# Weight splitting of four experts on two engines instead of three, and a later request for the words of the next conversion

## The chip, the core and the metric

The kernel runs on one core of a Trainium2 chip. A core has five engines that run their own instruction streams in order and wait for one another by semaphores: TensorE (PE, matmuls; PEld is its weight load), VectorE (DVE), ScalarE (ACT), GpSimd (POOL) and SyncE (SP, which here issues most of the DMAs). ACT issues some DMAs from its own stream, too. The metric is the device time of one execution in microseconds (us); the time of the kernel before is the median of three runs.

## What is computed

The reference is a chain of three blocks on 1536 tokens of 512 values, all in float32:

```
attn = softmax(scale * q k^T + bias, on global and local columns) v      # 2 x 8 heads, 768 x 64
x    = attn as (1536, 512)
e(i) = argmax(x w_gate); gate = softmax(x w_gate)[e(i)]                  # 8 experts, capacity 384
x[i] = gate * relu(x[i] w1[e(i)]) w2[e(i)]                               # 512 -> 1024 -> 512
out  = softplus(x w_in) w_out                                            # 512 -> 2048 -> 512
```

`w_in` and `w_out` arrive as 64-bit words and are turned into float32 by the kernel itself.

## The kernel before

The kernel runs three stages one after the other: attention with routing (up to about 147 us), the eight experts (147 to 358 us) and the dense layer, called m here (358 to 627 us). The order of the instructions on each engine is the order in which the Python code emits them; nothing moves them afterwards.

**Experts.** The experts run in order of their number of tokens, as use index `ui` 0 to 7, with 256, 352, 272, 240, 224, 208, 200 and 184 columns. Each has eight steps `f`. A step emits `e_stage1` (matmuls into `ps_h`, then a relu that makes the hidden tile) and then, two steps behind (`LAG = 2`), `e_stage2` (matmuls into `ps_y`). For experts 1 to 4 (`SPLIT`) every operand is held as two parts of a narrower type, a high part and a low part, and `three` (L1116 to L1118) makes three matmuls of each product. There the relu is ACT's `hs` (L1143), and DVE makes the low part of `hs` (L1144). After the last step of an expert `e_out` copies its result out: `zh` on ACT (L1174), `zl` on DVE (L1175), four each. `trans_x` transposes the next expert's tokens (`ps_xt`), with `xTs` in two parts (ACT L1110, DVE L1111).

**Splitting the weights.** Weights of experts 1 to 4 (key "s") and of the dense layer (key "m") come as 512 KB `raw` tiles, four buffers. `split` takes them in pieces of 128 x 512: the high part is a cast (`hi`, L441 or L443), the low part is `raw - hi` (L431). Four pieces make one use, which is what PE needs for two steps, a pair. In the kernel before, every fourth high part is a DVE cast (L441), the other three are ACT's (L443); every fourth low part is DVE's, the other three are POOL's. `pump` calls `split` once per step and then issues the loads of freed `raw` buffers on SP.

**Converting the words.** `conv_step` runs in every second step of the experts, in every step of the dense layer, and at heads 6 and 7 of the later attention tiles. One call stores the result of the call before the last, finishes the one before (DVE L81) and starts a new one: ACT reads the words `cr` (`csq`, L77), and DVE reads them twice (L78, L79). `cr` has three buffers. At the end of the same call `conv_load` requests the next words (L495): on ACT's queue up to the end of the experts, on SP's in the dense layer. Since the three buffers are all taken, that request goes into the buffer that the same call has just begun to read, so the engine that issues it waits for DVE's L79.

Of the kernel before, what the change touches and what calls it, by code (L numbers as in the profile page):

```python
# [72 lines left out]
def words_to_f32(nc, t, u, hi, lo, step):  # L73

    if step == 0:

        nc.scalar.activation(u, hi.bitcast(F32), AF.Abs, scale=2.0 ** -112)  # L77
        nc.vector.tensor_scalar(t, lo, 29, None, op0=ALU.logical_shift_right)  # L78
        nc.vector.scalar_tensor_tensor(t, in0=hi, scalar=-0x80000000, in1=t, op0=ALU.bitwise_and, op1=ALU.bitwise_or)  # L79
    else:  # L80
        nc.vector.scalar_tensor_tensor(t, in0=u.bitcast(I32), scalar=3, in1=t, op0=ALU.logical_shift_left, op1=ALU.bitwise_or)  # L81
# [225 lines left out]
def fast_path(ctx, tc, q, k, v, n_global, n_local, w_gate, w1, w2, cap, w_in, w_out, out, const):  # L307
    nc = tc.nc
# [113 lines left out]
    npiece, nhi = [0], [0]  # L422
    halfway = deque()

    def split(done, n):
        for _ in range(n):
            if halfway:
                raw, hi, lo, last = halfway.popleft()
                npiece[0] += 1
                eng = nc.vector if npiece[0] % 4 == 0 else nc.gpsimd  # L430
                eng.tensor_tensor(lo, raw, f32(hi), op=ALU.subtract)  # L431
                freed[0] += last
            if pending and pending[0][-1] <= done:
                raw, key, bi, k, c, _ = pending.popleft()
                if k == 0 and c.start == 0:
                    wq[key] = (wpool.tile([P, 2, NC, FQ], F32R, name="w1s", tag=f"b{bi}1", bufs=1),
                               wpool.tile([P, 2, FQ // P, DM], F32R, name="w2s", tag=f"b{bi}2", bufs=1))
                hi, lo = (wq[key][k][:, x, c, :] for x in range(2))
                nhi[0] += 1
                if nhi[0] % 4 == 0:  # L440
                    nc.vector.tensor_copy(hi, raw)  # L441
                else:
                    nc.scalar.copy(hi, raw)  # L443
                halfway.append((raw, hi, lo, c.start > 0))

    conv_done = [0]

# [5 lines left out]
    def pump(done, n, parts=1, most=NRAW):  # L453


        held[0] -= freed[0]
        freed[0] = 0
        split(done, n)
        while held[0] < most:
            if not rawq:  # L460
                if not loads_q or not ready(loads_q[0][0]):
                    return
                if loads_q[0][0][0] == "e":
                    if not parts or loads_q[0][2] > done:
                        return
                    parts -= 1
                start_load(*loads_q.popleft())
                continue
            src, key, bi, k, after = rawq.popleft()
            nb = src.shape[1]  # L470
            raw = rpool.tile([P, 1024], F32, name="raw", tag="raw", bufs=NRAW).rearrange("p (c f) -> p c f", c=nb)
            nc.sync.dma_start(raw, src)
            held[0] += 1
            for h in range(2):
                c = slice(h * nb // 2, (h + 1) * nb // 2)
                pending.append((raw[:, c, :], key, bi, k, c, after))
# [9 lines left out]
    conv_raw = deque()  # L486
# [4 lines left out]
    def conv_load():  # L491
        if conv:
            src, dst = conv.popleft()
            raw = cv.tile([P, FQ, 2], I32, name="cr", tag="cr", bufs=3)
            conv_q[0].dma_start(raw.rearrange("p n w -> p (n w)"), src)  # L495
            conv_raw.append((raw, dst))

    def conv_step(n):

        for _ in range(n):  # L500
            if conv_out:
                dst, t = conv_out.popleft()
                nc.sync.dma_start(dst, f32(t))
                conv_done[0] += 1
            if conv_now:
                dst, t, u = conv_now
                words_to_f32(nc, t, u, None, None, 1)
                conv_out.append((dst, t))
                conv_now.clear()
            if conv_raw:  # L510
                raw, dst = conv_raw.popleft()
                t = cv.tile([P, FQ], I32, name="ct", tag="cq", bufs=4)
                u = cv.tile([P, FQ], F32, name="csq", tag="cu", bufs=2)
                words_to_f32(nc, t, u, raw[:, :, 1], raw[:, :, 0], 0)
                conv_now.extend([dst, t, u])
                conv_load()


    ident = const.tile([P, P], F32, name="ident")
# [437 lines left out]
    last = len(tiles) - 1  # L957
# [13 lines left out]
    for n in range(NH + 8):  # L971
# [19 lines left out]
        if n < NH:  # L991
            if h == 1:
                load(i + 2)
            if h == (1 if i else 3):
                prep(i + 1, 0)
            if h % 2 and (i or h > 4) or i and h == 2:
                zero_fill(1)
            if h == (3 if i else 5):
                prep(i + 1, 1)
            if h == 5:  # L1000
                load_v(i + 2)
            if h == 6 and i in (2, 3, 4):
                conv_load()
            if h == 7:
                dup(i + 1)
                prev_v(i + 1)
                if i >= 5 and len(sc_q) > (i > 10):
                    scatter_x()
            if i >= 5 and h >= 6 and i < last:
                conv_step(1)  # L1010
# [174 lines left out]
    for s in range(len(steps) + LAG):  # L1185
        if s < len(steps):
            ui, f = steps[s]
            e_stage1(ui, f)
            if f in (3, 5, 6):
                trans_x(ui + 1, (3, 5, 6).index(f))  # L1190
            if f == 7 or s == 0:
                if s == 0:
                    load_order()
                load_x(ui + 1 + (f == 7))
        if s >= LAG:
            ui, f = steps[s - LAG]
            e_stage2(ui, f)
            u = part(ui, f)[0]
            if f == NFE - 1 or part(ui, f + 1)[0] != u:
                done = u  # L1200
        pump(done, 3 if s > 2 else 0, s % 2 == 0)
        if 1 <= s <= 4:
            next(routed, None)
        if s >= 6 and s % 2 == 0:
            conv_step(1)
# [78 lines left out]
    for x in range(len(plan)):  # L1284
        m_stage1(x)
        if LAG <= x < len(plan) - TAIL + LAG:
            m_stage2(x - LAG)
            if (x - LAG) % 2 == 1:
                done = plan[x - LAG][2]
        conv_step(1)  # L1290
        pump(done, 2)
        if x < NTT:
            scatter_ids(x)

        if x == 2 * NTT:
            nc.sync.dma_start(ids_row, ids_d.rearrange("(j p) o -> j (p o)", p=P))
        if x == 2 * NTT + 4:
            nc.vector.tensor_copy(ids_f, ids_row)
        if x == 2 * NTT + 5:
            ps = bank("D", "ps_ids")  # L1300
            nc.tensor.transpose(ps[:, :NTT], ids_f, ident[:NTT, :NTT])
            nc.vector.tensor_copy(ids_sb, ps[:, :NTT])
        if x == 2 * NTT + 2:
            slow = nc.values_load(slow_i[0:1, 0:1], min_val=0, max_val=1,
                                  skip_runtime_bounds_check_because="one minus a minimum of comparisons")
# [47 lines left out]
```

## Time and profile before

| | us |
|---|---|
| median of 3 runs (632.97 to 636.32) | 634.72 |
| the profiled execution | 634.79 |
| its span on the core | 633.0 |
| PE busy in the span | 606.7 |
| DVE, ACT, POOL busy | 366.9, 274.0, 171.0 |
| mean granted clock of TensorE, as a share of full speed | 0.989 |

Busy times of PE are of pipelined matmuls: a matmul of 0.27 us can start 0.11 us after the one before. A gap in PE's row is therefore a little shorter than the time that was lost. "issue" as the end of a wait means that the profile shows no other engine for it. Where rows name a line, it is that of the kernel before; from L501 on, lines of the changed kernel are up to two higher.

### The profile page before, as it was taken

The numbers are of one execution on the slowest core, as the hardware profiler recorded it, in microseconds if no ns is written. First come the engines' busy times: TensorE is split into PE (matmuls) and PEld (weight loads), VectorE is DVE, ScalarE is ACT, GpSimd is POOL, SyncE is SP. The second block draws the span as 40 slices with busy tenths as digits, with TensorE's granted clock in tenths as the row PEclk, the third lists the DMA queues.
The fourth block names the chain that finished last, engine by engine and source line by source line (L and its number), as shares of the span: only waits on it lengthen the run. The fifth ranks groups of instructions, "written<-read, shape, count | busy, mean of one in ns | idle before, by whom it ended". The sixth has DMA issues, their size and how long they took to land. (4 is left out here: it accounts for less than half of the span.)

```text
span 633.0 us, 10187 instructions
## 1 busy us (share of the span) xinstructions
PE 606.7 (96%) x3514; PEld 535.8 (85%) x3514; DVE 366.9 (58%) x1007; ACT 274.0 (43%) x600; POOL 171.0 (27%) x186
## 2 busy tenths in 40 slices
PE   6999999999999998889999999999999999999996
PEld 4899889898899997789999978888888878888874
DVE  7766888854776677733157495454577532333451
ACT  4565666743444434323253454444444433433340
POOL 4231544220755455500044241112022200100201
PEclk9999999989999999979999999999999999999998
DMA  8867778914776676779964534546422000000101
GB/s 158 225 168 215 188 213 234 316 70 134 248 229 203 213 216 191 219 262 379 376 230 133 158 71 81 134 68 80 128 66 85 2 0 1 33 34 2 50 19 70
DMA packets 92695, 93.37 MB, mean 148 GB/s; under 512 B 43314, under 2 KB 63818, under 8 KB 92634
## 3 DMA queue, kind: packets, MB, share of 16 engines
q1 hardware_dynamic: 83850, 74.53, 42.4%
q10 hardware_dynamic: 6480, 11.80, 5.5%
q0 software_dynamic: 2304, 6.30, 2.6%
q8 instruction: 30, 0.49, 0.3%
q14 instruction: 31, 0.25, 0.2%
HBM read 72.15 MB, written 20.46 MB: 146 GB/s over the span
## 5 line engine op out<-in xcount | busy, mean ns | idle before, releaser
L431 POOL TENSOR_TENSOR w1s<-raw,w1s 128x512 fp32r<-128x512 f32 x48 | 64.2, 1358 | 176.2 <-ACT w1s L443 172.0
L1228 DVE SCALAR_TENSOR_TENSOR sa<-ps_m,sa 128x512 f32<-128x512 f32 x48 | 33.1, 690 | 116.7 <-ACT sa L1227 116.7
L1225 ACT ACTIVATE sa<-ps_m 128x512 f32<-128x512 f32 x48 | 28.8, 600 | 139.8 <-PE ps_m L1118 139.8
L1116 PE MATMUL ps_m<-zh,w1s 128*128 128x512 f32 x192 | 76.1, 396 | 1.1 <-DVE sa L1228 1.1
L1117 PE MATMUL ps_m<-zl,w1s 128*128 128x512 f32 x192 | 75.7, 394 | 0.0
L1118 PE MATMUL ps_o<-w2s,g 128*128 128x512 f32 x192 | 75.7, 394 | 0.0
L1117 PE MATMUL ps_o<-w2s,g 128*128 128x512 f32 x192 | 75.5, 393 | 0.0
L1118 PE MATMUL ps_m<-zh,w1s 128*128 128x512 f32 x192 | 75.4, 392 | 0.0
L1116 PE MATMUL ps_o<-w2s,g 128*128 128x512 f32 x192 | 74.8, 389 | 0.0
L747 ACT ACTIVATE s_sb<-s_sb,negm 128x232 f32<-128x232 f32 (+1 forms) x96 | 44.0, 473 | 37.1 <-DVE negm L740 25.5
L731 PE MATMUL ps_s<-kwin,qpad 128*128 128x232 f32 (+1 forms) x192 | 55.8, 377 | 1.7 <-DVE negm L740 1.5
L1167 PE MATMUL ps_y<-h,w 128*128 128x256 f32 (+3 forms) x256 | 51.0, 343 | 0.0
L1140 PE MATMUL ps_h<-xT,w 128*128 128x256 f32 (+3 forms) x256 | 50.9, 343 | 0.0
L1140 PEld LDWEIGHTS ps_h<-xT,w 128*128 128x128 f32 x256 | 44.5, 190 | 1.9 <-ACT xT L1095 0.2
L1167 PEld LDWEIGHTS ps_y<-h,w 128*128 128x128 f32 x256 | 44.1, 190 | 1.4
L1116 PEld LDWEIGHTS ps_m<-zh,w1s 128*128 128x128 f32 x192 | 36.1, 188 | 10.7 <-DVE sa L1228 2.3
L1116 PE MATMUL ps_y<-hs,w2s 128*128 128x352 f32 (+3 forms) x128 | 39.2, 306 | 5.0 <-DVE zl L1175 5.0
L1275 POOL DMA_INDIRECT out_dram<-o,ids_sb x12 | 11.7, 973 | 117.4 <-DVE o L1270 53.3
L1117 PEld LDWEIGHTS ps_o<-w2s,g 128*128 128x128 f32 x192 | 36.0, 188 | 8.7
L1116 PE MATMUL ps_h<-xTs,w1s 128*128 128x352 f32 (+3 forms) x128 | 38.7, 302 | 4.9 <-DVE hs L1144 4.9
L1116 PEld LDWEIGHTS ps_o<-w2s,g 128*128 128x128 f32 x192 | 36.1, 188 | 8.4 <-DVE g L1235 0.3
L1118 PEld LDWEIGHTS ps_m<-zh,w1s 128*128 128x128 f32 x192 | 36.0, 188 | 8.4
(207 smaller groups left out, 1377.1 us busy)
## 6 DMA issues: line engine op xcount, KB each, us to landing
w<-in_moe_w_dram SPq DMA_DIRECT2D x16, 1024.0 KB
raw<-in_moe_w_dram SPq DMA_DIRECT2D x32, 512.0 KB
cr<-in_moe_w_in_dram ACTq DMA_DIRECT2D x24, 256.0 KB
xs_d<-early SPq DMA_DIRECT2D x22, 256.0 KB
cr<-in_moe_w_out_dram ACTq DMA_DIRECT2D x21, 256.0 KB
wi_d<-ct SPq DMA_DIRECT2D x32, 128.0 KB
wo_d<-ct SPq DMA_DIRECT2D x32, 128.0 KB
raw<-wi_d SPq DMA_DIRECT2D x8, 512.0 KB
```

Of the source, the lines that this page charges most:

```text
L431: eng.tensor_tensor(lo, raw, f32(hi), op=ALU.subtract)
L731: nc.tensor.matmul(ps[:, :w], tr[i][h % 2][:, h // 2, :], kwin[t % 2][:, h // 2, c0:], start=True, stop=True)
L747: nc.scalar.activation(pt_[n][:, :w], pt_[n][:, :w], AF.Exp, bias=negm[:, n:n + 1], scale=-1.0)
L1116: nc.tensor.matmul(ps, hi_l, hi_r, start=first, stop=False)
L1117: nc.tensor.matmul(ps, hi_l, lo_r, start=False, stop=False)
L1118: nc.tensor.matmul(ps, lo_l, hi_r, start=False, stop=last)
L1140: nc.tensor.matmul(ps, w[:, c, js], x[:, c, :], start=c == 0, stop=c == NC - 1)
L1167: nc.tensor.matmul(ys[ui, d], w[:, j, sl], h, start=f == 0, stop=f == NFE - 1)
L1225: nc.scalar.activation(a, ps, AF.Abs)
L1228: nc.vector.scalar_tensor_tensor(a, in0=ps, scalar=0.0, in1=a, op0=ALU.max, op1=ALU.add)
L1275: nc.gpsimd.indirect_dma_start(out=out, out_offset=bass.IndirectOffsetOnAxis(ap=ids_sb[:, 4 * c + t:4 * c + t + 1], axis=0), in_=o, in_off ...
```

## The change

Three edits, in two functions.

- `split`: the low parts of "s" weights all go to DVE, their high parts all to ACT. "m" weights are shared out as before. POOL then has no instruction between the routing and the dense layer's first weights.
- `conv_step`: the request for the next words moves from the end of the call to its start, so it is issued one call later and into a buffer that was read by the call before.
- The key travels with the piece in `halfway`, so that `split` knows its kind.

```diff
             if halfway:
-                raw, hi, lo, last = halfway.popleft()
+                raw, hi, lo, last, key = halfway.popleft()
                 npiece[0] += 1
-                eng = nc.vector if npiece[0] % 4 == 0 else nc.gpsimd
+                eng = nc.vector if key[0] == "s" or npiece[0] % 4 == 0 else nc.gpsimd
                 eng.tensor_tensor(lo, raw, f32(hi), op=ALU.subtract)
...
-                if nhi[0] % 4 == 0:
+                if key[0] == "m" and nhi[0] % 4 == 0:
                     nc.vector.tensor_copy(hi, raw)
                 else:
                     nc.scalar.copy(hi, raw)
-                halfway.append((raw, hi, lo, c.start > 0))
+                halfway.append((raw, hi, lo, c.start > 0, key))
...
     def conv_step(n):
 
         for _ in range(n):
+            if conv_raw and len(conv_raw) < 3:
+                conv_load()
             if conv_out:
...
                 conv_now.extend([dst, t, u])
-                conv_load()
```

What stands in a row on ACT in one pair of expert 3 (240 columns), before; `hs` opens a step, `cr` is the request of the next words, `csq` the read of the present ones:

```order
L1143 ACTIVATE hs<-ps_h 128x240
L1110 CAST xTs<-ps_xt 128x4x128
L443 CAST w1s<-raw 128x512 x2
L443 CAST w2s<-raw 128x512
L1143 ACTIVATE hs<-ps_h 128x240
L77 ACTIVATE csq<-cr 128x256
L495 DMA cr<-in_moe_w_in_dram 128x512
L1143 ACTIVATE hs<-ps_h 128x240
```

The same place of the changed kernel:

```order
L1144 ACTIVATE hs<-ps_h 128x240
L1111 CAST xTs<-ps_xt 128x4x128
L443 CAST w1s<-raw 128x512 x2
L443 CAST w2s<-raw 128x512
L1144 ACTIVATE hs<-ps_h 128x240
L443 CAST w2s<-raw 128x512
L495 DMA cr<-in_moe_w_in_dram 128x512
L77 ACTIVATE csq<-cr 128x256
L1144 ACTIVATE hs<-ps_h 128x240
```

A fourth cast of a high part has come to ACT, and the request stands ahead of the read instead of behind it.

On DVE the same pair before:

```order
L1144 SCALAR_TENSOR_TENSOR hs<-ps_h,hs 128x240
L1111 TENSOR_TENSOR xTs<-ps_xt,xTs 128x4x128
L1144 SCALAR_TENSOR_TENSOR hs<-ps_h,hs 128x240
L441 CAST w2s<-raw 128x512
L431 TENSOR_TENSOR w2s<-raw,w2s 128x512
L81 SCALAR_TENSOR_TENSOR ct<-csq,ct 128x256
L78 TENSOR_SCALAR ct<-cr 128x256
L79 SCALAR_TENSOR_TENSOR ct<-cr,ct 128x256
```

and in the changed kernel:

```order
L1145 SCALAR_TENSOR_TENSOR hs<-ps_h,hs 128x240
L1112 TENSOR_TENSOR xTs<-ps_xt,xTs 128x4x128
L431 TENSOR_TENSOR w1s<-raw,w1s 128x512 x2
L1145 SCALAR_TENSOR_TENSOR hs<-ps_h,hs 128x240
L431 TENSOR_TENSOR w2s<-raw,w2s 128x512 x2
L81 SCALAR_TENSOR_TENSOR ct<-csq,ct 128x256
L78 TENSOR_SCALAR ct<-cr 128x256
L79 SCALAR_TENSOR_TENSOR ct<-cr,ct 128x256
```

DVE's cast is gone and three low parts have come: two in the first step of the pair, one in the second. On POOL the 48 low parts of "s" weights are gone and nothing is added.

In the attention, at heads 6 and 7 of a late tile, ACT has before (`s_sb` is the exponential of a head, `pT` a copy of its transposed scores):

```order
L747 ACTIVATE s_sb<-s_sb,negm 128x232
L77 ACTIVATE csq<-cr 128x256
L495 DMA cr<-in_moe_w_in_dram 128x512
L747 ACTIVATE s_sb<-s_sb,negm 128x232
L765 COPY pT<-ps_pt 128x512
L77 ACTIVATE csq<-cr 128x256
L495 DMA cr<-in_moe_w_out_dram 128x512
L811 COPY xTr<-ps_xT 128x512
```

and in the changed kernel:

```order
L748 ACTIVATE s_sb<-s_sb,negm 128x232
L495 DMA cr<-in_moe_w_in_dram 128x512
L77 ACTIVATE csq<-cr 128x256
L748 ACTIVATE s_sb<-s_sb,negm 128x232
L766 COPY pT<-ps_pt 128x512
L495 DMA cr<-in_moe_w_in_dram 128x512
L77 ACTIVATE csq<-cr 128x256
L812 COPY xTr<-ps_xT 128x512
```

Each request has moved ahead of the read in its call, and it fetches what the call before fetched until now. PE's order is the same in both kernels.

## Rows read from the trace of the kernel before

**Rows 1.** The page, part 1: busy us (share of the span), instructions.

```profile
PE 606.7 (96%) x3514; PEld 535.8 (85%) x3514; DVE 366.9 (58%) x1007; ACT 274.0 (43%) x600; POOL 171.0 (27%) x186
```

**Rows 2.** Windows: stretch, length, busy us and instructions per engine, clock, DMA share, GB/s.

```profile
230.00:260.00 30.00, 24.34 (x207) 23.55 (x206) 21.22 (x35) 12.09 (x30) 16.11 (x13) 1.00 0.73 216
260.00:290.00 30.00, 25.75 (x203) 25.37 (x202) 14.88 (x34) 7.84 (x22) 5.57 (x5) 0.89 0.78 266
```

**Rows 3.** Windows of PE alone, 270 to 280 us: busy, clock, DMA share, GB/s.

```profile
272.00:274.00 2.00, 2.00 (x11) 0.50 1.05 378
276.00:278.00 2.00, 2.00 (x12) 0.50 0.32 114
```

**Rows 4.** Waits of PE, 172 to 290 us: total us, times, longest.

```profile
PE ps_y L1116 <- DVE zl L1175: 5.0, 2, 2.6
PE ps_h L1116 <- DVE hs L1144: 4.9, 4, 1.7
```

**Rows 5.** Timeline of ACT, expert 3: start, length, line, tiles, [idle before <-releaser].

```profile
250.65 0.63 ACT L443 CAST w2s<-raw 128x512 fp32r<-128x512 f32 x1
...
251.43 0.45 ACT L77 ACTIVATE csq<-cr 128x256 f32<-128x256 f32 x1
255.92 0.34 ACTq L495 DMA_DIRECT2D cr<-in_moe_w_in_dram  x1
256.31 0.37 ACT L1143 ACTIVATE hs<-ps_h 128x240 fp32r<-128x240 f32 x1 [4.43 <-issue]
```

**Rows 6.** Timeline of DVE, the same pair.

```profile
251.91 1.24 DVE L441 CAST w2s<-raw 128x512 fp32r<-128x512 f32 x1
253.18 1.67 DVE L431 TENSOR_TENSOR w2s<-raw,w2s 128x512 fp32r<-128x512 f32 x1
254.77 0.41 DVE L81 SCALAR_TENSOR_TENSOR ct<-csq,ct 128x256 int32<-128x256 int32 x1
...
255.42 0.42 DVE L79 SCALAR_TENSOR_TENSOR ct<-cr,ct 128x256 int32<-128x256 int32 x1
256.71 0.41 DVE L1144 SCALAR_TENSOR_TENSOR hs<-ps_h,hs 128x240 fp32r<-128x240 f32 x1 [0.86 <-ACT hs L1143]
```

**Rows 7.** Timeline of PE, expert 3: first matmuls of half steps and after gaps.

```profile
246.26 0.27 PE L1116 MATMUL ps_h<-xTs,w1s 128*128 128x240 f32 x1
...
247.60 0.27 PE L1116 MATMUL ps_y<-hs,w2s 128*128 128x240 f32 x1
...
249.74 0.38 PE L1116 MATMUL ps_h<-xTs,w1s 128*128 128x240 f32 x1 [0.63 <-DVE hs L1144]
...
257.17 0.38 PE L1116 MATMUL ps_h<-xTs,w1s 128*128 128x240 f32 x1 [1.41 <-DVE hs L1144]
```

**Rows 8.** Timeline of DVE in expert 2: a low part with POOL at rest.

```profile
208.45 0.69 DVE L431 TENSOR_TENSOR w2s<-raw,w2s 128x512 fp32r<-128x512 f32 x1
```

**Rows 9.** Groups of DVE, 204 to 262 us: count | busy us, mean ns.

```profile
L1144 DVE SCALAR_TENSOR_TENSOR hs<-ps_h,hs 128x240 fp32r<-128x240 f32 x7 | 2.9, 408 | 7.5 <-ACT hs L1143 7.5
...
L1175 DVE TENSOR_TENSOR zl<-ps_y,zh 128x272 f32 x4 | 1.5, 430 | 0.0
L1111 DVE TENSOR_TENSOR xTs<-ps_xt,xTs 128x512 fp32r<-128x512 f32 x2 | 1.4, 692 | 0.1
```

**Rows 10.** Timeline of SP and of ACT at the first weight loads.

```profile
152.44 10.70 SPq L472 DMA_DIRECT2D raw<-in_moe_w_dram  x6
...
161.68 1.14 ACT L443 CAST w1s<-raw 128x512 fp32r<-128x512 f32 x2 [1.05 <-DMA raw<-in_moe_w_dram]
```

**Rows 11.** Timeline of ACT between heads 6 and 7 of attention tile 9.

```profile
110.97 0.49 ACT L747 ACTIVATE s_sb<-s_sb,negm 128x232 f32<-128x232 f32 x1 [2.21 <-issue]
```

**Rows 12.** Timeline of PE: the same transposes at head 7 of tiles 4, 5, 9, 10.

```profile
56.66 0.61 PE L809 MATMUL ps_xT<-ident,x 128*128 128x128 f32 x4
67.33 0.61 PE L809 MATMUL ps_xT<-ident,x 128*128 128x128 f32 x4
...
109.88 0.60 PE L809 MATMUL ps_xT<-ident,x 128*128 128x128 f32 x4
121.22 0.60 PE L809 MATMUL ps_xT<-ident,x 128*128 128x128 f32 x4
```

## The prediction

> **What bounds the kernel now.** I read the shares of busy time first: PE is busy for 606.7 of 633.0 us [rows 1], and the profiled execution took 634.79 us, 0.07 above the median of the runs, so 1.8 us lie around the span and the sum is made against 634.79. A kernel that is filled by PE gains only where PE stands still or runs slowly. So the second view is the one by stretches: of the 60 us from 230 to 290 PE is busy for 50.1, and in the second half the granted clock is 0.89 [rows 2]. That is 9.9 us of rest, the whole of it in experts 3 and 4. The third view splits the clock: from 272 to 278 us PE got 0.50, the lower of its two levels (1.2 instead of 2.4 GHz), just behind the last of the gaps, and then the full clock again [rows 3]. Third, who ends the gaps: DVE alone, six times, 9.9 us: four times `hs`, twice `zl` at the change of experts [rows 4].
>
> The timelines say why DVE is late. In one pair of expert 3, ACT starts `csq` at 251.43, is done at 251.88, and issues the next request only at 255.92; its `hs` starts at 256.31 after 4.43 us of rest [rows 5]. In that time DVE does its cast (1.24), its low part (1.67) and the three conversion instructions, whose last ends at 255.84 [rows 6]: that is what the request waited for, since its buffer is the one that L79 reads. Then ACT's `hs`, DVE's `hs` at 256.71, and PE goes on at 257.17 [rows 7]. So ACT and DVE work by turns, and the turn takes 7.43 us (249.74 to 257.17). PE's own work is 1.34 us for 12 matmuls [rows 7], 5.36 for the 48 of a pair. In expert 1 PE needs longer than 7.43 (352 columns against 240), in expert 2 about 6.1, so the backlog grows through expert 2 and becomes gaps from expert 3 on.
>
> **The request at the next call.** Removed: ACT's wait of 4.4 us in each pair. In the new place the request's buffer was read by the call before, one pair earlier, and that L79 stands ahead on DVE of everything that the present pair asks of it; I put its wait at nothing. What is queued behind it on ACT is only `csq` and then `hs`. If the cover were gone (DVE a whole pair behind), ACT would wait again, but PE would then be held by DVE itself.
>
> The price is a shorter lead: words come two calls ahead of their use instead of three. No read of the words waits for a DMA anywhere in the trace. The nearest row for a landing time: of six weight requests from 152.44 on, the third is what ACT waits for until 161.68, at most 9.2 us with 2 MB in flight [rows 10]. Two calls in the experts are two pairs, 10.7 us at 5.36. Between nothing and, say, 1 us for each of the eight calls of the saturated stretch behind 280 us, I take nothing. The Trainium skill ("DMA: Bandwidth & Descriptors", "Rules for kernel authors") says to issue a DMA early and to wait for it late, which speaks against this edit; by it one would keep three calls of lead and expect the words to be late, and the rows show a lead that still covers the longest landing.
>
> On SP, in the dense layer, the request moves ahead of the store and of the weight loads in its step; there it no longer waits for the present L79, so what is queued behind it starts sooner. PE has no gap there that it could close; I put it at nothing.
>
> **The low parts on DVE, the high parts on ACT.** Per pair, DVE loses a cast (1.24) and a low part of 1.67 [rows 6] and gets four low parts. With POOL at rest a low part took 0.69 on DVE in the middle of the experts [rows 8]. After the change POOL has nothing to do there, so I take 0.69 for all, 2.76 a pair against 2.91 before; the other end is 1.67, 6.7 a pair. DVE's pair in expert 3 is then two `hs` of 0.41, four low parts 2.76, the conversion 1.07 (254.77 to 255.84), `zl` 0.43 (four per expert, one per pair) and `xTs` 0.69 in half the pairs, 0.35 [rows 6, 8, 9]: 0.82 + 2.76 + 1.07 + 0.43 + 0.35 = 5.43 us, against 5.36 of PE and its transposes. Instructions of DVE overlap: L81 starts at 254.77, and the low part ahead of it ends at 254.85 [rows 6]. With some 0.08 for each of nine instructions the pair takes 4.7 us. So DVE keeps up in expert 3 with 12% to spare, and easily in experts 1 and 2. The Trainium skill ("VectorE: DVE Perf Modes", "The DRAIN you can't avoid") says that the next instruction doesn't start before the pipeline is empty; by that the pair is the full 5.43, and four pairs of expert 3 would cost PE 0.3 us in all; the row of L81 shows it otherwise.
>
> ACT gets a fourth cast of 0.63 [rows 5] in place of its wait. It was busy for 12.09 us in 30 [rows 2], in about four turns: 3.0 each, 3.6 with the cast, 5.36 to hand. PE's stage 1 of a step needs `hs` of two steps before to be out of PSUM, three half steps (4 us) after it was computed; ahead of it in ACT's row stand at most three casts (1.9 us), in DVE's two low parts and the conversion (2.5 us). No gap there. At the change of experts four `zh` and four `zl` must pass within about a half step; before, they stood behind the request. I leave 0.5 us for the two places together. POOL's rest costs nothing: its 48 low parts go, and it issues no DMA in that stretch.
>
> Weight loads of experts 5 to 7 come after the gain of time; DMA share is 0.73 and 0.78 at 216 and 266 GB/s [rows 2], and 378 GB/s was reached [rows 3]. What experts 1 to 4 need in 5.4 instead of 7.4 us is 216 x 7.4 / 5.4 = 296 GB/s, below that.
>
> **The attention.** ACT waits 2.21 us there in front of an exponential, behind the request [rows 11]. The period of a tile was 10.67 us before the first conversion and 11.34 with one [rows 12]. With three full tiles of the late kind at most 3 x 0.67 = 2.0 us can come back, at the least nothing: DVE's own conversion work stays, and between heads 6 and 7 the new request still waits for the L79 of one head earlier. I take 1.0.
>
> **The sum.** Gaps 9.9 us [rows 4]. Each gap is longer than it looks: a matmul of 0.27 is followed after 0.11 (1.34 / 12), so 0.16 is hidden in its length, and the first one behind a gap takes 0.38, 0.11 more [rows 7]; six times 0.27 is 1.6. The clock: 0.11 of 30 us, 3.3 [rows 2]; without gaps I see no reason for it to fall. Attention 1.0, left over at the changes of expert -0.5. Together 15.3 us: 634.8 - 15.3 = 619.5.
>
> **Rivals.**
>
> A gap remains and the clock falls again. The last gap was a `zl` wait of up to 2.6 us, and the lower clock came behind it. If `zl` still waits behind the two low parts of its step, half of the 5.0 us stays (2.5), and the clock costs 3.3 again; late words or a DVE at 5.43 add up to 1. Then 619.5 + 6.3 = 626. For it: DVE's margin is small. Against it: both engines come out of the wait of 4.4 us a pair. Chance 0.17.
>
> Low parts do not get faster: what made one take 1.67 is not POOL's work but, say, ACT's cast beside it. Then DVE's pair is 5.43 + 4 x 0.98 = 9.35 us and DVE is the bound. Against the present turn of 7.43 that is 1.9 us for each of eight pairs of experts 2 and 3 and, against 7.7 us of PE, 1.65 for each of the four of expert 1: 22 us more, and the clock no better: 634.8 + 22 - 1 = 656. It decides from a low part of (7.43 - 2.67) / 4 = 1.19 us on. Against it: 0.69 in the experts' own stretch [rows 8]. Chance 0.06.
>
> The wait changes its name. DVE's work per pair is about what it was, 2.76 for 2.91; if DVE and not ACT's wait sets the turn, PE waits for DVE as before: 633 to 636. Against it: DVE is busy for 21.22 of 30 us [rows 2], and it rests in front of `hs` for ACT [rows 6, 9]. That the request still waits would end the same. Chance 0.08.
>
> **How the numbers follow.** The forecast, 616 to 622.5 around 619.5, gets 0.69; its lower end has all of the attention's 2.0 and some hidden losses that are not in the six gaps. The range for 8 in 10 reaches up into the first rival: 615 to 627. About 0.5% (3.2 us) is what a measurement of this kernel can tell from no change. Faster: 0.69 + 0.17 = 0.86; same: 0.08; slower: 0.06.
>
> **What would show it.** Right: no "issue" or L79 wait in front of ACT's `hs`; low parts of 0.69; PE without gaps from 230 on, clock 1.00 there; expert 5 starting about 15 us sooner; DVE busy for over 80% in expert 3. Wrong: low parts near 1.67; PE waiting for `hs` or `zl` at each pair; ACT's `csq` waiting for a DMA; a lower clock in any stretch of the experts; expert 5's matmuls waiting for their weights.

## The result, and the profile of the changed kernel

The changed kernel takes 618.59 us (median of 4 runs, 617.88 to 619.73), the kernel before 634.84 beside it (4 runs, 632.97 to 636.32): a ratio of 0.9747, 95% interval 0.9716 to 0.9779. The forecast was 619.5. The profiled execution of the changed kernel took 619.25 us, its span is 617.5.

The page, part 1, of the changed kernel (busy us, share of the span, instructions), to set against [rows 1]:

```profile
PE 600.8 (97%) x3514; PEld 534.5 (87%) x3514; DVE 365.3 (59%) x1039; ACT 288.7 (47%) x616; POOL 107.6 (17%) x138
```

DVE's busy time is almost what it was, though 32 more instructions stand in it: its low parts have become short. Windows of the changed kernel over experts 2 to 4 and the start of expert 5 (columns as in [rows 2]):

```profile
204.00:230.00 26.00, 26.00 (x204) 26.00 (x203) 20.26 (x43) 15.94 (x35) 0.00 (x0) 1.00 0.70 222
230.00:253.00 23.00, 23.00 (x205) 23.00 (x205) 19.80 (x43) 15.38 (x35) 0.00 (x0) 1.00 0.84 254
253.00:275.00 22.00, 22.00 (x199) 22.00 (x198) 10.72 (x30) 7.33 (x20) 0.00 (x0) 1.00 0.89 330
275.00:290.00 15.00, 15.00 (x97) 14.97 (x96) 3.97 (x12) 4.95 (x13) 0.00 (x0) 1.00 1.05 382
```

PE has no rest and the full clock in each of them, where [rows 2] had 9.9 us of rest and 0.89. In expert 3 (second line) DVE is busy for 19.80 of 23.00 us, 86%.

The timeline of ACT in one pair of expert 3 (start, length, line, tiles, [idle before <-releaser]), the counterpart of [rows 5]:

```profile
241.43 0.62 ACT L443 CAST w2s<-raw 128x512 fp32r<-128x512 f32 x1
242.60 0.37 ACT L1144 ACTIVATE hs<-ps_h 128x240 fp32r<-128x240 f32 x1 [0.55 <-PE ps_h L1119]
242.68 0.34 ACTq L495 DMA_DIRECT2D cr<-in_moe_w_in_dram  x1
242.86 0.61 ACT L443 CAST w2s<-raw 128x512 fp32r<-128x512 f32 x1
243.37 0.44 ACT L77 ACTIVATE csq<-cr 128x256 f32<-128x256 f32 x1
245.29 0.37 ACT L1144 ACTIVATE hs<-ps_h 128x240 fp32r<-128x240 f32 x1 [1.48 <-PE ps_h L1119]
```

The request is issued while `hs` runs, and what ACT waits for in front of `hs` is PE: the order of who waits has turned round. The same pair on DVE:

```profile
243.32 1.28 DVE L431 TENSOR_TENSOR w2s<-raw,w2s 128x512 fp32r<-128x512 f32 x2
244.53 0.42 DVE L81 SCALAR_TENSOR_TENSOR ct<-csq,ct 128x256 int32<-128x256 int32 x1
244.86 0.29 DVE L78 TENSOR_SCALAR ct<-cr 128x256 int32<-128x256 int32 x1
245.18 0.42 DVE L79 SCALAR_TENSOR_TENSOR ct<-cr,ct 128x256 int32<-128x256 int32 x1
245.70 0.41 DVE L1145 SCALAR_TENSOR_TENSOR hs<-ps_h,hs 128x240 fp32r<-128x240 f32 x1
```

Two low parts take 1.28 us together. Over all experts, the groups of L431 on DVE (minimum/median/maximum in ns):

```profile
L431 DVE TENSOR_TENSOR w1s<-raw,w1s x32: 680/686/695, 158.4 to 252.6; 128x512 fp32r<-128x512 f32 x32
L431 DVE TENSOR_TENSOR w2s<-raw,w2s x32: 680/684/687, 160.6 to 255.0; 128x512 fp32r<-128x512 f32 x32
```

And the waits of PE from 150 to 620 us, in place of [rows 4], have a single line, in the dense layer:

```profile
PE ps_m L1117 <- DVE sa L1229: 1.1, 1, 1.1
```

Where the time came from is read best by stages, between the first matmuls of expert 1, of expert 5 and of the dense layer, and the last `ps_o`. In the changed kernel the first two of these are

```profile
171.65 0.51 PE L1117 MATMUL ps_h<-xTs,w1s 128*128 128x352 f32 x1
274.41 0.52 PE L1141 MATMUL ps_h<-xT,w 128*128 128x208 f32 x2
```

and the table gives the stages of every kernel of this study, worked out in this way from one profiled execution each (us):

| kernel | start of expert 1 | experts 1 to 4 | experts 5 to 7 | dense layer |
|---|---|---|---|---|
| before | 172.69 | 117.25 | 68.43 | 268.17 |
| changed | 171.65 | 102.75 | 68.43 | 268.13 |
| request_only | 172.83 | 103.49 | 69.64 | 268.14 |
| split_only | 172.56 | 102.76 | 70.06 | 268.23 |
| two_ahead | 169.73 | 103.49 | 69.04 | 268.14 |
| lead_one | 171.06 | 102.76 | 68.55 | 268.13 |
| extra1 | 171.92 | 102.76 | 68.88 | 268.16 |
| extra3 | 171.66 | 110.16 | 68.43 | 268.11 |
| rest_apart | 172.32 | 102.75 | 70.40 | 266.79 |
| after_again (changed, again) | 172.17 | 102.73 | 68.62 | 268.12 |
| heads_apart | 174.07 | 102.76 | 68.84 | 268.15 |
| late_lows | 174.50 | 102.76 | 68.46 | 267.05 |
| both_apart | 169.93 | 102.76 | 69.02 | 266.79 |

Of the 15.56 us between before and changed, 14.50 are in experts 1 to 4 and 1.04 ahead of them. The first column moves by almost 5 us between executions whose code is nearly the same, and goes in part with the granted clock of the attention (0.96 in late_lows, 1.00 in both_apart, below); the other columns repeat within 0.2 us where no wait differs. So a change inside the experts is read from the second column to a tenth of a microsecond, and a change of one microsecond in the attention can't be read from the first column at all.

### The profile page after: what moved, and what is told of

Same layout as the page of the kernel before. It is cut to its first block, busy times and chain, and to the rows that moved or that the text cites. A ratio compares the mean times of both kernels' runs of the same rounds, so it can differ in the third digit from the quotient of the medians.

```text
span 617.5 us, 10175 instructions
## 1 busy us (share of the span) xinstructions
PE 600.8 (97%) x3514; PEld 534.5 (87%) x3514; DVE 365.3 (59%) x1039; ACT 288.7 (47%) x616; POOL 107.6 (17%) x138
## 5 line engine op out<-in xcount | busy, mean ns | idle before, releaser
L431 POOL TENSOR_TENSOR w1s<-raw,w1s 128x512 fp32r<-128x512 f32 x16 | 23.2, 1468 | 228.3 <-ACT w1s L443 228.3
L1118 PEld LDWEIGHTS ps_o<-w2s,g 128*128 128x128 f32 x192 | 36.0, 188 | 8.6
L1117 PEld LDWEIGHTS ps_o<-w2s,g 128*128 128x128 f32 x192 | 36.2, 188 | 8.4 <-DVE g L1236 0.3
L1119 PEld LDWEIGHTS ps_o<-w2s,g 128*128 128x128 f32 x192 | 36.0, 188 | 8.0 <-DVE g L1237 0.4
L1118 PEld LDWEIGHTS ps_m<-zl,w1s 128*128 128x128 f32 x192 | 36.0, 188 | 7.7
L1237 DVE TENSOR_TENSOR g<-sa,g 128x512 fp32r<-128x512 f32 x48 | 38.1, 793 | 1.7
```

Source lines behind the costliest of these rows:

```text
L1117: nc.tensor.matmul(ps, hi_l, hi_r, start=first, stop=False)
L1118: nc.tensor.matmul(ps, hi_l, lo_r, start=False, stop=False)
L1119: nc.tensor.matmul(ps, lo_l, hi_r, start=False, stop=last)
L1237: nc.vector.tensor_tensor(gl_, a, f32(gh), op=ALU.subtract)
```

## The experiments

The theory from the prediction: the request makes ACT wait for DVE's L79 within each pair, ACT and DVE work by turns of 7.43 us, and that is what PE's gaps and the low clock behind them come from. Its rival: DVE's work sets the turn, and without shorter low parts the waits only change their names. The first two kernels take one edit each.

**request_only**: before, with the request at the start of the call.

```diff
         for _ in range(n):
+            if conv_raw and len(conv_raw) < 3:
+                conv_load()
...
                 conv_now.extend([dst, t, u])
-                conv_load()
```

> The request of the next words moved to the start of the call, the splitting as in the kernel before (one low part in four on DVE, one high part in four on DVE, POOL busy). Theory A, ACT's wait behind the request sets the turn of ACT and DVE: the wait of 4.4 us a pair is gone although DVE's low part still takes about 1.66 us beside POOL; DVE's pair is then 0.82 + 1.24 + 1.67 + 1.07 + 0.43 + 0.35 = 5.6 us at most, near PE's 5.4 to 5.5, so most of the gain is there: 619 to 622 us, gaps of PE in experts 3 and 4 under 1 us, clock 1.00. Theory B, the slow low parts on DVE set the turn and POOL's rest gives the gain: 630 us or more, gaps as before.

Measured: 620.88 us (619.31 to 622.36; ratio 0.9793, 0.9748 to 0.9839). Beside POOL the low parts on DVE still take up to 1.67 us in this kernel, though fewer of them do (median 1.17 us against 1.66 in before), and PE has hardly a gap. The group of L431 on DVE in before and then in request_only, and the waits of PE in request_only, 150 to 345 us:

```profile
L431 DVE TENSOR_TENSOR w2s<-raw,w2s x16: 683/1660/1668, 161.0 to 267.4; 128x512 fp32r<-128x512 f32 x16
```

```profile
L431 DVE TENSOR_TENSOR w2s<-raw,w2s x16: 683/1167/1666, 160.2 to 256.9; 128x512 fp32r<-128x512 f32 x16
```

```profile
PE ps_xt L1107 <- DMA xr<-xs_d: 1.0, 1, 1.0
PE ps_h L1117 <- DVE hs L1145: 0.5, 1, 0.5
```

One gap of 0.5 us is left of 9.9. The rival falls: DVE with its old instructions keeps up, once ACT does not wait for it. New is a wait for the tokens of expert 7 (`xr`); more on it below.

**split_only**: before, with the other two edits and the request in its old place.

```diff
-                eng = nc.vector if npiece[0] % 4 == 0 else nc.gpsimd
+                eng = nc.vector if key[0] == "s" or npiece[0] % 4 == 0 else nc.gpsimd
...
-                if nhi[0] % 4 == 0:
+                if key[0] == "m" and nhi[0] % 4 == 0:
```

> The splitting as in the changed kernel (POOL at rest in experts 1 to 4), the request left at the end of its call. Theory A: ACT still waits for L79 in every pair, but DVE's way to L79 is shorter by 1.24 + 1.67 - 2 x 0.69 = 1.5 us, so the turn falls from 7.4 to about 5.9 us: enough for expert 2 (about 6.1 us of PE), 0.4 us short in each pair of expert 3; 621 to 625 us, waits of ACT for issue or L79 of 2 to 3 us, the attention as before. Theory B: as the changed kernel but for the attention, 619 to 620 us, and no gap.

Measured: 621.48 us (619.81 to 623.03; 0.9808, 0.9760 to 0.9857). Experts 1 to 4 take 102.76 us, as with both edits. ACT's wait is still there, half as long, as its timeline in expert 3 shows (lines as in the kernel before):

```profile
238.62 0.66 ACT L443 CAST w2s<-raw 128x512 fp32r<-128x512 f32 x1
239.13 0.49 ACT L77 ACTIVATE csq<-cr 128x256 f32<-128x256 f32 x1
241.49 0.34 ACTq L495 DMA_DIRECT2D cr<-in_moe_w_in_dram  x1
241.87 0.37 ACT L1143 ACTIVATE hs<-ps_h 128x240 fp32r<-128x240 f32 x1 [2.25 <-DVE ct L79]
```

2.25 us in place of the 4.43 of [rows 5], mostly since the cast and the long low part (1.24 + 1.67) in front of L79 have become two low parts (1.28). No gap follows from it. The time lies in the range of theory A by luck: the 0.4 us that A had expected to be short in each pair of expert 3 did not come, and what is lost against the changed kernel stands elsewhere, 1.6 us in experts 5 to 7, of which a wait for `xr` is 1.4, and 0.9 ahead of expert 1. So either edit alone closes the gaps of the experts: 13.8 us by the request, 14.5 by the splitting, 14.5 by both. They are not two gains to be added; each takes enough out of the same turn.

**two_ahead**: before with one number left out: two requests ahead of the first call instead of three, so that the request in its old place finds a free buffer.

```diff
-            if h == 6 and i in (2, 3, 4):
+            if h == 6 and i in (3, 4):
```

> The kernel before with one request fewer ahead: two instead of three at heads 6 of tiles 3 and 4, so the request at the end of a call, in its old place behind the read, goes into a buffer that nobody reads. Nothing else differs. Theory A (it is the buffer just read that makes the request wait, not its place in the order): 619 to 622 us, as with the request moved. If the place behind the read is what costs, or words come late with a lead of two: above 625 us.

Measured: 618.67 us (617.97 to 620.28; 0.9772, 0.9726 to 0.9817), a little below the expected range, experts 1 to 4 in 103.49, the same as request_only. It is the buffer that was just read that made ACT wait, not the place of the request in the call.

**lead_one**: the changed kernel with the words one call ahead instead of two, from the experts on.

```diff
+    conv_lead = [3]
...
-            if conv_raw and len(conv_raw) < 3:
+            if conv_raw and len(conv_raw) < conv_lead[0]:
...
+    conv_lead[0] = 2
```

> The changed kernel, with the words requested one call ahead instead of two from the experts on. Tests how much of the lead is needed. If words land within 4 to 6 us in experts 1 to 4, a lead of one pair (5.4 us or more) just covers them: at most 1 us of wait in a call there, PE without gaps; behind expert 4, where the DMA engines are full, up to 3 us of wait in each of eight calls in ACT's order. Theory A with slack on ACT: 618 to 623 us. If late words reach PE at once: 630 us or more.

Measured: 619.82 us (616.62 to 621.75; 0.9783, 0.9726 to 0.9841). Now ACT does wait for the words, in its waits from 150 to 345 us:

```profile
ACT csq L77 <- DMA cr<-in_moe_w_in_dram: 3.1, 2, 1.8
ACT csq L77 <- DMA cr<-in_moe_w_out_dram: 2.2, 2, 1.1
```

PE does not: experts 1 to 4 take 102.76. The lead that the edit costs is not needed; even the next call's distance is hidden by what ACT has in hand.

**extra1** and **extra3**: the changed kernel with the last low part of each pair in the experts made two and four times. The repeats write the same values again.

```diff
                 eng.tensor_tensor(lo, raw, f32(hi), op=ALU.subtract)
+                if key[0] == "s" and lo.shape[1] == 1 and last:
+                    for _ in range(1):
+                        eng.tensor_tensor(lo, raw, f32(hi), op=ALU.subtract)
```

> The changed kernel with one low part in each pair made twice on DVE (the last piece of a use). DVE's pair in expert 3 goes from 4.7 to 5.4 us by start to start, to 6.1 by full lengths; PE needs 5.4 to 5.5. If instructions overlap as the timeline shows, the margin is just used up and the time stays within 1 us of the changed kernel, 617 to 620 us. If the full lengths counted, expert 3 would lose 0.6 us in each of four pairs: 621 us or more.

Measured: 619.44 us (618.22 to 620.00; 0.9757, 0.9726 to 0.9787), experts 1 to 4 in 102.76: one more low part in each pair costs nothing.

> The changed kernel with the last low part of each pair made four times on DVE. DVE's pair: 4.7 + 3 x 0.62 = 6.6 us in expert 3 and about 6.8 in expert 2 by start to start, against 5.5 and 6.3 of PE and 7.9 in expert 1. If DVE is next to set the time: four pairs of expert 3 lose 1.1 us each, four of expert 2 about 0.5, together 6 us less what the two steps of lead swallow (up to 4): 620 to 626 us, gaps of PE for hs or zl again in expert 3, and 3 us more if the clock falls behind one. If DVE had room to spare: 619 us.

Measured: 627.29 us (625.22 to 630.51; 0.9896, 0.9857 to 0.9936), experts 1 to 4 in 110.16, 7.4 us more. The whole is 1.3 us above the range that was expected without a lower clock: expert 3 takes 26.67 us, expert 4 25.64, against 22.71 and 22.20 in the changed kernel, and expert 2, which was to lose 2 us, lost nothing (25.84 in both). What DVE is behind comes out later than was expected, in expert 4. The waits of PE, 150 to 300 us, and windows of this kernel:

```profile
PE ps_y L1120 <- DVE zl L1179: 3.6, 2, 1.9
PE ps_h L1120 <- DVE hs L1148: 2.0, 3, 1.0
```

```profile
231.00:258.00 27.00, 24.11 (x206) 23.32 (x205) 26.45 (x55) 15.76 (x36) 0.00 (x0) 1.00 0.71 229
258.00:285.00 27.00, 24.10 (x209) 23.72 (x208) 15.38 (x39) 7.90 (x21) 0.00 (x0) 1.00 0.89 314
```

DVE is full (26.45 of 27.00 us) and PE waits for it at the same places as in [rows 4]: DVE is the next bound, and the changed kernel stands between one and three low parts per pair away from it. The turn of a pair in expert 3 is 26.67 / 4 = 6.67 us. The start-to-start count of the prediction, 4.7 us and three more low parts at some 0.61, gives 6.5, and DVE's pairs there, from one first `hs` of a pair to the next, take 6.8 and 6.7 us (7.6 in the pair with the four `zl`); the sum of full lengths, 5.43 + 3 x 0.69 = 7.5, would give 30 us for the expert. The clock stays at 1.00 behind these gaps, unlike behind the last of those of before.

**rest_apart**: the changed kernel with two attempts on what is left of the waits: the dense layer's low parts all on DVE as well, so that POOL has none beside the long L78 at 351 us (shown at the end), and the attention's conversion steps at heads 3 and 6 of a tile. **after_again** is the changed kernel itself on the same chip.

```diff
-                eng = nc.vector if key[0] == "s" or npiece[0] % 4 == 0 else nc.gpsimd
+                eng = nc.vector
...
-            if i >= 5 and h >= 6 and i < last:
+            if i >= 5 and h in (3, 6) and i < last:
```

> A try for more: the changed kernel with all low parts on DVE in the dense layer too (POOL then only scatters there), and with the two conversion calls of an attention tile at heads 3 and 6 instead of 6 and 7. The one gap of PE in the dense layer (1.3 us, behind a DVE instruction of 3.3 us beside POOL's low parts and scatter) should go, and up to 0.4 us in each of four late attention tiles: 1 to 3 us below the changed kernel, 615.5 to 618 us. If DVE then is too full in the dense layer: gaps there, 620 us or more.

> The changed kernel once more, on the same chip as the try for more, to compare the two: 617.5 to 620 us.

Measured: after_again 618.87 us (618.37 to 620.71; 0.9759, 0.9732 to 0.9786), rest_apart 622.72 (620.53 to 625.03; 0.9819, 0.9793 to 0.9845): it was to be faster and is not. The dense layer did become 1.3 us shorter, the gap at 354 us is gone. Lost were 1.8 us in experts 5 to 7. The two profiled executions are only 0.6 us apart (620.53 and 619.91), so most of the 3.9 us between the medians lies in no trace; the mean granted clock was 0.985 to 0.994 in the six runs of rest_apart and 0.994 to 0.997 in the five of after_again. POOL's timeline shows what else moved: with no low part in front of them, the scatters of `ids` (L933), which start at 350 us in the changed kernel, run from 161 us on, twelve of them up to 253 us.

```profile
161.43 1.16 POOL L933 DMA_INDIRECT ids_d<-tokid,pos_i  x1 [14.64 <-DVE pos_i L928]
168.07 0.97 POOL L933 DMA_INDIRECT ids_d<-tokid,pos_i  x1 [5.47 <-DMA ids_d<-tokid,pos_i]
...
252.91 1.26 POOL L933 DMA_INDIRECT ids_d<-tokid,pos_i  x1 [8.45 <-DMA ids_d<-tokid,pos_i]
```

Beside them every transfer lands later. The DMA issues from 170 to 255 us (count, KB each, median us from issue to landing), first of rest_apart, then of the changed kernel:

```profile
raw<-in_moe_w_dram SPq DMA_DIRECT2D x24, 512.0 KB, 8.4
wo_d<-ct SPq DMA_DIRECT2D x8, 128.0 KB, 7.0
ids_d<-tokid,pos_i POOLq DMA_INDIRECT x10, 8.5
```

```profile
raw<-in_moe_w_dram SPq DMA_DIRECT2D x23, 512.0 KB, 4.1
wo_d<-ct SPq DMA_DIRECT2D x8, 128.0 KB, 4.7
```

The weights take 8.4 instead of 4.1 us (4.5 and 4.9 in late_lows and after_again, which have no scatter there either) while the rate is the same (244 GB/s in both). The wait of PE for the tokens of expert 7 is 1.8 us here:

```profile
PE ps_xt L1107 <- DMA xr<-xs_d: 1.8, 1, 1.8
```

**heads_apart**, **late_lows**, **both_apart** take the two attempts apart. Heads_apart is the changed kernel with the second edit of rest_apart alone. In late_lows the first four uses of the dense layer's low parts stay on POOL, which holds the scatters back, and the rest go to DVE; both_apart has that and the heads.

```diff
-                eng = nc.vector if key[0] == "s" or npiece[0] % 4 == 0 else nc.gpsimd
+                eng = nc.vector if key[0] == "s" or npiece[0] % 4 == 0 or npiece[0] > 80 else nc.gpsimd
```

> The changed kernel with the attention's conversion steps at heads 3 and 6 of a tile instead of 6 and 7. Tells the two edits of rest_apart apart. If the scatters of ids on GpSimd slowed that kernel: no scatter before 350 us here, the attention's last ps_xT 0 to 1.5 us sooner, time 617 to 619.5. If it was the attention's conversions at other heads: 621 to 624 as in rest_apart.

> The changed kernel with the low parts of the dense layer's weights from the 81st piece on (those from about 349 us on) on VectorE, the first four uses' on GpSimd as before, so that the scatters of ids cannot start before about 340 us. Theory (L78 took 3.33 us beside GpSimd's low part, and rest_apart lost its time to the early scatters): the gap of 1.25 us at 354 us goes, experts 1 to 5 within 103 us, time 617 to 618.5. Rival (the low parts on VectorE themselves cost rest_apart its time): 620 or more.

> Both edits together. If they add and the early scatters were rest_apart's loss: 616 to 618.5. If rest_apart's loss has another cause: 620 to 623.

Measured: heads_apart 622.01 us (619.67 to 622.74; 0.9796, 0.9766 to 0.9826), late_lows 618.45 (615.94 to 622.17; 0.9746, 0.9711 to 0.9782), both_apart 617.67 (616.44 to 619.77; 0.9744, 0.9716 to 0.9772).

By the medians heads_apart points to the heads as rest_apart's loss, and both_apart, with the same heads, denies it. The stages explain it: experts and dense layer of heads_apart are those of the changed kernel within 0.4 us, and its expert 1 starts 2.4 us later. The window of the attention in late_lows, where nothing differs from the changed kernel up to there, and in both_apart:

```profile
0.00:172.00 172.00, 160.98 (x1129) 147.77 (x1130) 122.18 (x582) 99.77 (x237) 48.48 (x90) 0.96 0.69 191
```

```profile
0.00:172.00 172.00, 162.12 (x1153) 147.57 (x1154) 122.62 (x588) 101.74 (x241) 47.49 (x90) 1.00 0.72 201
```

The granted clock was 0.96 in the one and 1.00 in the other, and expert 1 starts at 174.50 and 169.93. Heads_apart had 0.96 as well. Whether the moved conversions make the lower clock more frequent stays open: the three kernels with them were at 0.96, 0.98 and 1.00 in their traces. What holds without the clock is the dense layer: 268.1 us with POOL's low parts beside it, 267.05 and 266.79 without them from 349 us on, and the wait for `sa` is gone. Both_apart and rest_apart differ in the engine of the first four uses' low parts and, through it, in when the scatters run; experts 5 to 7 took 69.02 and 70.40 us, and most of these 1.4 us is the longer wait for `xr` (0.4 and 1.8). That the early scatters make it longer is not shown: the last of them runs at 253 us, those tokens are requested at 302, and split_only waits 1.4 us for them without any early scatter. Of the 3.8 us between these two profiled executions the start of expert 1 (169.93 and 172.32) is the larger part. So why rest_apart is slower stays open in the main. None of the three is shown to beat the changed kernel: the interval of both_apart is nearly that of the result.

## Why the prediction was right

The forecast was 619.5, the result is 618.59, and the terms of the sum hold one by one, the one for the attention only in part.

**Gaps, hidden losses, clock: 14.8 less 0.5 for what is left at the changes of expert, 14.3 together.** Experts 1 to 4 became 14.50 us shorter. The bound named was right: the gaps were worth 9.9 us in the waits' column, and the small correction for overlapping matmuls and the clock's 3.3 us were both needed to come to 14.5. The 0.5 us that I left for `zl` did not arise: PE has no wait for it, and 14.8 stands against 14.5.

**The request.** Its wait at its new place was put at nothing; in the changed kernel no `hs` waits for anything but PE. Two_ahead shows the mechanism by itself. The lead of two calls was said to suffice; lead_one shows that one does, with 5.3 us of waits on ACT that do not reach PE. In the changed kernel the words landed in 2.9 to 6.6 us from the experts on; the bound taken from the weights was 9.2. The rule of the Trainium skill that was weighed there ("DMA: Bandwidth & Descriptors", "Rules for kernel authors") has a condition that this case brings out: a request is early only if its buffer is free, and the earlier request of before bought its lead with 4.4 us a pair on the engine that issued it.

**The low parts.** 0.69 was taken, 0.684 and 0.686 measured, and none of the 64 in the experts took over 0.695, though ACT's casts ran beside them; so the second rival falls, too. The pair of 4.7 us on DVE against 5.43 by full lengths was the closest call of the prediction; extra1 would have shown the latter as a loss, and extra3's 6.67 us agree with the former. What the Trainium skill says of the pipe ("VectorE: DVE Perf Modes", "The DRAIN you can't avoid") doesn't hold here as a sum of lengths; the same section adds that an instruction which is not held starts earlier, and the page's section "Two Vector instructions with no wait between them" says when one is held. This case's rows agree with the earlier start: in the pair above L81 and L78 start 0.07 and 0.09 us before the instruction ahead ends; L79, which reads what L78 writes, starts 0.03 us after it.

**What the prediction did not see.** It costed the two edits as parts of one gain and never asked what each would do alone. Either alone is enough, since a turn of 7.43 us has to lose only some 1.75 us to be hidden behind PE (a pair of expert 3 takes 22.71 / 4 = 5.68 us with its transposes; the prediction took 5.36). Its third rival, that the wait only changes its name, rested on DVE's work being the bound; request_only shows that DVE's old work alone was no bound either.

**The attention.** 1.0 us was taken, and expert 1 starts 1.04 us sooner in the trace; this agreement is luck, since that start moves by several microseconds between executions. ACT's wait in front of the exponential, 2.21 us in [rows 11], has gone, as its timeline between heads 6 and 7 of tile 9 shows:

```profile
108.07 0.36 ACTq L495 DMA_DIRECT2D cr<-in_moe_w_in_dram  x1
108.47 0.44 ACT L77 ACTIVATE csq<-cr 128x256 f32<-128x256 f32 x1
109.33 0.49 ACT L748 ACTIVATE s_sb<-s_sb,negm 128x232 f32<-128x232 f32 x1 [0.42 <-DVE negm L741]
```

What this is worth shows in single tiles. The transposes of [rows 12] at tiles 9 and 10 in the changed kernel:

```profile
110.01 0.61 PE L810 MATMUL ps_xT<-ident,x 128*128 128x128 f32 x4
120.72 0.50 PE L810 MATMUL ps_xT<-ident,x 128*128 128x128 f32 x3
```

Between them lie 10.71 us. In before they are 11.34 us apart and in split_only, which also has the wait, 11.27; in the seven other kernels without the wait and with the conversions at the same heads they are 10.70 to 10.77. From tile 5 to 6 it is 9.82 and 9.73 us with the wait and 9.21 to 9.26 without, from tile 10 to 11 10.53 and 10.54 with it and 9.98 to 10.08 without. So the 0.67 us for each of three tiles, which the prediction had as its upper end, nearly came back, 1.6 to 1.8 us in all. What the prediction lacked is that the tiles between lose and gain by other waits: from tile 6 to 8 it is 21.60 and 21.45 us in before and split_only and 21.00 to 24.08 in the eight others, where PE waits for POOL's `vp` in five of them, 0.6 to 1.8 us, and the clock falls to 0.91 between 80 and 100 us in two (extra3 and late_lows). From the first to the last `ps_xT` it is therefore 114.94 and 114.84 us with the wait and anything from 112.30 to 115.80 without. What makes `vp` late was not tried. That wait in the changed kernel, in the waits of PE from 76 to 101 us:

```profile
PE ps_pv L780 <- POOL vp L583: 0.6, 1, 0.6
```

**The room that was called sufficient.** For the DMAs the prediction compared 296 GB/s with the 378 that had been reached, and for experts 1 to 4 that was right. Behind expert 4 it was too easy: from 275 to 290 us the queues are full (382 GB/s, DMA share 1.05), and the tokens of expert 7, requested at about 300 us, landed up to 1.8 us too late in some kernels (experts 5 to 7: 68.43 us at best, 69.04 in two_ahead, 69.64 in request_only, 70.06 in split_only). The two traces of the changed kernel list no such wait (68.43 and 68.62). This, and DVE at 86%, are the next limits.

**Rivals.** No gap and no lower clock remained in the experts, so the first didn't come about. Its price for the clock was too rigid, though: extra3 has gaps of up to 1.9 us at the same places and kept the full clock.

## What to carry to other kernels

Before moving work between engines, look for a request that is issued behind the read of its own buffer: with as many requests in flight as there are buffers, it makes its engine wait for the slowest reader, and one request fewer in flight can be worth more than the lead. Two cures for one turn don't add; take each alone to learn which slack is left over. When an engine is freed of work, see what its queue held back, since that now runs earlier, beside other transfers. And compare stages, not whole times, when the clock of an untouched stage moves the whole by several microseconds.

## What was unexpected of the hardware

- **Small scatters slow large loads.** Twelve scatters of 128 rows with 4 bytes each, one at a time, about doubled the landing time of 512 KB loads on another queue (8.4 us in the one trace that has them there, 4.1, 4.5 and 4.9 in three that don't) at about the same rate, 243 to 244 GB/s.
- **DVE beside POOL.** The one wait that is left in the dense layer comes from an instruction of 0.29 us that took 3.33. The timelines of DVE and of POOL in the changed kernel:

```profile
351.07 3.33 DVE L78 TENSOR_SCALAR ct<-cr 128x256 int32<-128x256 int32 x1
```

```profile
350.43 1.25 POOL L933 DMA_INDIRECT ids_d<-tokid,pos_i  x1 [0.16 <-issue]
351.70 1.31 POOL L431 TENSOR_TENSOR w1s<-raw,w1s 128x512 fp32r<-128x512 f32 x1
352.95 1.29 POOL L431 TENSOR_TENSOR w2s<-raw,w2s 128x512 fp32r<-128x512 f32 x1
```

It ends 0.16 us behind POOL's last low part. The Trainium skill ("SBUF — State Buffer", "Who interferes with whom") says that the two engines share a pair of ports, and that a DVE instruction in a 2-port mode and one of GpSimd block each other for the length of the one that was issued first. In which mode L78 runs no run here shows; its row starts beside the scatter and ahead of both low parts, and still it ends behind them. A low part of DVE's, which has two inputs, took 1.67 us beside POOL in before (253.18 to 254.85) and ended 0.55 us behind POOL's (252.82 to 254.30); whether it ran slowly or was held until then the rows don't tell. Late_lows, without POOL's low parts there, has 1.36 us as its longest L78 and no wait of PE.
- **The clock of the attention.** With the same code up to there it was granted 0.96 to 1.00 in different executions, and expert 1 started 3.4 us apart (171.06 in lead_one at 1.00, 174.50 in late_lows at 0.96). What decides it was not tried.
